# A residual block on one core: 36 scalings go from VectorE to ScalarE, with a new order of operations

## The chip, the core and the metric

The kernel runs on one core of a Trainium2 chip. The core has a matrix engine (TensorE, in the profile PE, with its weight loads as PEld), VectorE (DVE), ScalarE (ACT), GpSimd (POOL) and SyncE (SP), which issues most DMAs here. Each engine works through its own instructions in the order in which they were written, and waits on semaphores for the others. The metric is the device time of one execution in microseconds (us), the median of several runs. The profile is of one execution.

## What is computed

A residual block of a diffusion model, on x of shape (2, 512, 64, 64) in bfloat16:

```
def conv3(z, w):                     # 3x3, padded by 1, 512 -> 512 channels
    zp = jnp.pad(z, ((0, 0), (0, 0), (1, 1), (1, 1)))
    taps = [jnp.einsum("bchw,oc->bohw", zp[:, :, i:i+H, j:j+W], w[:, :, i, j])
            for i in range(3) for j in range(3)]
    ...
h = conv3(_silu(gn(x, g1, be1)), w1)
emb = _silu(t_emb) @ w_emb
h = h + emb.reshape(B, C, 1, 1)
h = conv3(_silu(gn(h, g2, be2)), w2)
return x + h
```

gn is a group normalization with 4 groups of 128 channels.

## The kernel before

**Stages.** A convolution ("layer") is done in chunks: layer, image and half of the rows. So there are eight, chunks 0 to 3 for the first convolution (two images, two halves) and 4 to 7 for the second. Each chunk has four units, one for each 128 output channels; `unit(c, k)` (line 818) writes unit k of chunk c, called u00 to u73 below, 32 in all.

**Input side.** For each chunk and each of the four input channel tiles, `load_a` (645) brings the half image (name a), `silu` (669) applies normalization and SiLU on ACT, and `rows_a` (680) and `rows_b` (694) form "row planes", sums and differences of every fourth row, mostly on DVE (names k, row and rob, with chunk and tile: rob23 is tile 3 of chunk 2). This saves multiplications: a convolution over rows is computed from six products, s = 0 to 5, in place of twelve. From chunk 1 on columns are treated likewise ("nested" products, A and B matmuls over 256 columns, beside plain ones over 512). Products of the following chunk's planes are formed while the units of this chunk run. The planes lie in two sets of buffers, one for each of two chunks.

**Output side.** PE sums the products of a unit in PSUM banks. ACT moves them to SBUF (`evac_o`, `evac_m`, `evac_pair`, `evac_b`, lines 842 to 858; names o4, o5, m0 to m3, b). DVE then adds the halves (names S and A), and the end of `unit` (1002 to 1015) turns four products into four rows:

```
tt(tw(SD, 1024), M(0, 2), M(2, 2), AD, nm + "s")
tt(M(0, 2), M(2, 2), M(0, 2), SB_, nm + "d")
se = CFG["s"][c]
scal(se[0], M(2), M(1), 8.0, nm + "8")
scal(se[1], M(3), M(1), 2.0, nm + "2")
scal(se[2], A(SD + 512, [[1, 512]]), A(SD + 1024, [[1, 512]]), 4.0, nm + "4")
```

The sums s and d, then three scalings by 8, 2 and 4 (128x512 elements each), then the additions y, on DVE. `scal` (373) takes ScalarE (`act`, line 371 in the profile) or VectorE (`ts`, line 352), as `CFG["s"]` says for each chunk. An accumulating DMA on POOL adds the outer rows (name oa). In the first layer the unit goes to a scratch tensor in DRAM (st), is squared and summed on ACT (sq), and `gn2` makes the second normalization's scale; in the second layer it is added by DMA to a copy of x in the output (names out and pre).

**Other work.** `prep_w1` and `prep_w2` make the transformed weights with scalings on ACT and sums on DVE, `fetch_w2` and `stream_w2` bring them; `emb` is the small matmul of the embedding; `stats1` sums and squares the second image on ACT (st10 to st13, in chunk 0). At the start `warm` and `fill` are matmuls whose results are not used, and st00 to st03 are the statistics of the first image.

**The order.** Nothing is emitted directly. Each helper records an operation in a `Plan` with its engine, the regions it reads and writes and so the operations before it. `ORDER` (168) is a string of 2753 two-character numbers, one for each operation, and `emit` (97) writes the operations in that order. The DMAs on SP and the work on POOL stand in it too, and each engine takes its operations in the sequence that results. So all instructions of the helpers have one line each in the profile: L348 is a DVE sum or difference, L352 a DVE scaling, L371 an operation of ACT, L386 a DMA, L390 a memset, L401 a matmul.

Of the kernel before, what the change touches and what calls it, by code (L numbers as in the profile page):

```python
# [165 lines left out]


ORDER = (
    "0D0E0F0G0H0I0R0S0T0U0W2T1u0v0y1Q2J1N2c3F1r2M0c0X0a0Z0Y0d0e0f00010b020g13030h14150i0j0k0l0L0m170n0N16180405061907"
    "081X1Y1Z1A1_0o1a1c0K1B0M1C1D0p0O1E1b1F1d0q0r1e0s1f0_1g1G1H2021231I1h090A0B0V0C3K1i0J22240t0u0w250x0z1j1J2610271k"  # L170
    "2e12281K292U1l2A1T2B1m1n112C1o2D1x2E2F1U2G1y2P1z1-1W0-1L1M1O1P1R1S1p1q1s1t1v1w2H2I2K2L2N2O3C3D3E3L0Q2Q1V2R2S0P3M"
    "4g2W2l2X2m2Y2n3G2Z4T3g4L2f3O2i3P3N3Q2h3S3R2g3V2a3H3a3W3U2o2p3h3i2q2r2s2t2u2v2w2x2y2z3j2-3u4M2d2j4N2k2_304U2b3Z32"
    "314O5P3X3k3c3d3b5H3Y3T4h4P5I4Q5J4k4V334X4W4Y344Z35364b374a3e4S4R3f384d4m4e4n4f6Y4j3v3w3x3y3z3-3_4243443l45464748"
    "494q4r4s4t3m41404B5Q4A6L4i4c5K6D5L5M6F6M6E4u4v3n3o4w4x4-4_50515253543p555c5d5e5f5h2V4l6Z5R3r6a5T7u5U5S5V3q5W5X7v"
    "5Z5a4p3s5N4C3t3I4D4G4F4E7w4H5b8y4o3J56395Y6GB7B84I3A4z574y3B6IB96H5g586N596P5B5C6O5A6Q5D6RBB6T6SBABD6U6K6W6J6X8z"
    "5O6V5i5j5k5l5m5n5o5r5s5t5u5w5x5y5z5-5_60616b6c6d6e6g5v5q5p6h6i6j6k6l6m6n6s6t6u6v6x6y6z6-6_70717262767763BC4JBN7h"
    "BF6fBP4KBH648-65A0686766BJA169A2BR5E8lBOBGBED56A5F6w7P78797A6o7B7C7D7x7y7z7-5G6p8081BQ828384858687BI74737EDDB47Q"
    "6q7RB57S6r7T7UB67V757W7XBL7FD7DF7YBK7ZBS7aBT7b7G7c7d7H7e7K7f7J7g7i8988D66BDEBM7ID97LDH7j7l8A7m7k7n8B7o7pD27tDL7M"
    "BUEeDN8C8D8EDG7_8F8H8I8J8K8L8M8N8O8S8T8U8V8W8X8Y8Z8_908GD88Q8P91929495969798999A9B9G9H9I9J9L9M9N9O9P9Q9R9S8a9W9X"
    "8m8b7O9p9q6CD37r8RD4DIDB7sDA8cDJ7N7q8d8n8f8p8o8q8g8r8e9C9D8t8s8hDP8v9KEgDKDMDC93DOEfEh9UAt9FEi9EDRDQ9T8x8w9V9Y9Z"  # L180
    "9a9b9c9d9f9eA3A4A5A6A8A9AAABACADAEAFAKALAMANAPAQARASATAUAVAWAaAbAcAdAeAfAgAhEm8u9r9t9s9u9v9w9x8iEuEo9gEjAG9hEqEn"
    "GB9yCrEwA7EpAHAuAO8kEk9k9j9-9i9_9l9zAXCsAYAiAjAvAIAxAwAyAJAzA-A_AZB0B2B3AkCQAlAoAnAmCRCtEvDSEl8jApEO9m9nAqCvB1Cw"
    "CuCxCTCyCzBVBWBXBYBaBbBcBdBZBiGDBjBeBfBgBhBlBmBnBoBtBuBvBwByBzB-B_C0C1C2C3C6C7C8C9CCCDCECFDTDUDVDW9oBkDYDZDaDbBp"
    "BqExBsEbEyEcCUBrEdE-EsErBxEPC5C4AsCAGJCGD0CVCSEzCWCBD1CHC_CIDcDdDeDfDjDkDlCXCYDmDrDsDtDuDwDXDhGLDgDxDyDzD-D_E0E1"
    "E4E5E6E7EAEBECEDF0F1F2F3FxEtE_GCGKDiCKCLG8CJC-G9GFGNCMCZGAArGRCaEQGEESERETGHEUGGEWEVDnDoDvGTGMFyE8E2E3EEGPDpDqCb"
    "EYE9GVHhHUHVGSHjGIEFEJEaCcEGEZEHGOCNCOEXHpHiGQGUF5F6F7F8F9FAFBFCFGFHFIFJFOFPFQFRFTFUFVFWFXFYFDEIGXHlCdGWEKCeFzFE"
    "FKFLF4HrFFHkHxHzFbFZFaFdFcFeFfFgFhFjFkFlFmGZGaGbGcGeGfGgGhGiGjGkGlFSGpGqGrGsGxGyGzG-H0H1H2H3FnH4H5H6H7HqGYHsCPF_"
    "CfG0F-G1CgG3G2ChFMFNCiHtCjFiCkG5FoHvClFpCmG7HmFqFsGmI3FrGuGoGtGnI5J6ELJ7G4HuHnFtG6HyHoI7GvHWKNGdHAHBHCHDHGHHHIHJ"
    "IBICH8ENH9FuI4EMHYHXHZH_HaCnCpHbCoHcGwCqHdHgHfHEG_HFHeHKI6KPJ8J9HwH-KONMNLFvHLIDIEIGIHIIIJIKILIMINIRISITIUIZIaIb"
    "IPIOIFIcIeIfIgIhIiIjIkIlIoIpIqIrIuIvIwIxIQJSJTJUJVJXJYJZJaI8HMIWHPHOIVI0HNI1I9JAHQIXIYImInIsJCJBJDJEItJFJGJJKQIy"  # L190
    "IdIzJHKRI-JKJIJ1IALeLfI2HRJLLgFwMvJ0KTI_KUKSJ2KVKWKXJMNJMwMxHSJWJgJfJbJcJdJeJiJjJkJlJqJrJsJtJmJhO-OzJvJwJxJyJzJ-"
    "J_K0K3JnNKK1K4K5K6K9KAKBKCKjKkKlKmKoKpKqKrKsKtKuKvKzK-K_L0JuK2KbKYLhLiJpJ3KaKZJNJoK7HTKDJ4QBQAOkJOLjLkJPLlLmK8Lo"
    "KELnKnKFKIKGKHLqLpKJKxL1KyKwMyL2MzLsL4L3JQM_KKN0OiOjL5L6L7L8LALBLCLDOxL9LELFLGLHLKLLLMLNLQLRLSLTLOLILJL-L_M0M1M3"
    "M4M5M6M7M8M9MAMEMFMGMHMMMNMOMPMRLUMSMTMUMVMWMXMYMbMcMdMeLPLrLVM-JRLWKcJ5N1M2MDMIMCMBN2LXLYLZN3LaKdKMMJMLMZMaMfN4"
    "N6MKN7MgLbPvRMKLPxRNPwLtOyMQOlMhMiMjMkNNNONPNQNSNTNUMlNVNWNXNYNZNbOHMmOmNRLdKeMnMqOIMoMpKfMrKgMsN5OKOoOLKhOpNaMu"
    "NcNdNeNgNhNiNjNkNlNmNnNrNsNtNuNvNwNxNyN-N_O0O1O2O3O4O5O_P0OqOMKiOnOJLuNoNpOrONP1P2P4NzP5P6P7NfOOOsLvOuNqLwOtPyP3"
    "O6LcSYQ8R7NFR5OPOwO7LxPzSZMtQ9TkR6N8P8P9PAPBPDPEPFPGTlP_R8O8OCPCNHQ0LyO9P-SHNGOBQ1LzRLRKOAPIPJPKPLPMPNPOPPPTPUPV"
    "PWPXPYPZPaPcPdPePfPgPhPiPHPQPjQCQDQEQFQHQIQJQKOvODQ2Q3PSPRPbPkQ4PlN9PmNAPnQLQMQNQOQQQRQSQTQVQWQXQYQZQaQbQcQgQhQP"
    "QiQjQkQlQmQnQpQqQrQsQtR9NBQ7RBRANCOFOEOGSJSIUwUxPpQGPoQUSKSWTTRCTVTUSXNINDRDPqQdQuQvQwRORPRQRRRTRUQ5NEQ6PrPtQoQx"
    "RVRWRXRYRZRaRcRdReRfRhRiRjRkRlRmRnRoPsREQfRFQeRGRHRbSLRJRITiW7SNSMSOSPRgRSQySQQzSRQ-SSSVUfTjUgUhPuRpR1Q_R0SUR2Rs"  # L200
    "RtRuRvRwRxRyRzR_S0S1S2S3S4S5S6SaXJSbS7R-ScSdSfSgShSiSjSkSlSmSoSpSqSrStSuSvSwSxSySzS-OQSTT2T3T4T5T6T7T8R3R4ORRqRr"
    "OSSnS8OTS9OUSAOVOWOXOYOZOaObSDSCSBSEOcOdOeOgS_OfT1OhSeT9TBTCTDTETFTGTHTITmTnToTpTrTsTtTATJTWSsT0TKTLTXTZTMTaTOTb"
    "TNUiTuTvTwTxTyT-T_U0U1U3U4U5U6U7U8U9UAUEUFUGTzUHUIUJUKULUNUOUPUQUBSFTqU2XIUvUuURUSUTUUUyUzU-U_V1V2V3V4V5V6V7V8VA"
    "VBVCVDTYYXSGW6YYVtTPTcTdTQUMVFVGVHVIUVVJVKVLVMVQVRVSVTTeTgUjUDTfUlUCUkUmUnUWThUXUoUpUbUqUYUsVrVsVuV9X1W5TRW4XGX3"
    "X2UaUZVNVvUrVxVwUtUcVyVPYFZnXHZmV0YDVEVUVVVWVXVZVaVbVcVdVeVfVgW8W9WAWBWDWEWFWGWHWIWJWKWMWNWOVYVzVhX4UdTSYEb0a_Ue"
    "YGWPWRWSWTWUWVWWWXWYWcWdWCYWWQVOWLWeWfWgWhWiWjWlWmWnWoWpWqWrWsXKXLWZV_V-ViW0W3X5VjX7W2X6X8W1VkZSZUX9VlVmXBXAVnXC"
    "YHXFXEVoYJWkWtWaWbYKYIYLXDWuYMWvYNWwWzVpYVZTajcKcLXMXNXPXQXRXSXTXUXVXWXYXZXaXbXdXeXfXgXhXiXjXkXoXpXqXXXrXsXtXuXv"
    "XxXyXzX-X_Y0Y1Y2ZVXcXOWxWyXlYQW-YOXmXnY3XwYUY4YRZWY5ZYY6YTYPZZZXahZlVqZkaiakY7Y9Y8ZaYZYaYbYcdcW_YeYfYgYhYiYjYkYl"
    "YnYoYpYqYsYtYuYvYwYxYyYzZ1Z2Z3Z4YmZ5Z6Z7Z8ZAZBZCZDZEZFY-YdZGZHZoZpZqZrZtbwdba-byX0bxazYAYBZ9YrZuZvZwZxZyZzZ-a0a1"
    "a2a3a5a6a7a8a9etesZIaAaBaCaGaHYCZbZcY_Z0ZdZgZJZiZKalanZLZeaobzaIaJaKaLaMaNZ_aPaQaRZMaSaTaUaVaWZNZOaDZsa4ZjapZfam"  # L210
    "ZPaXaOarZhaqaEaFasauaYavb-aZc0aab_atc1acabadaeZQb1b2b3b4b6b7b8b9bAbBbCbDbFbGbHbIbKbLbMbNbObPbQbRbVbWbXbYbEc2ayaf"
    "cDc4c3YSc7c8cCc6bZbabbbSbJcHbcbdbebfbgbhbibjbkblcMcNbmcOcPcQcRcScTcVcWcXcYcZcacbcccgchcicjckclbTbUcUcEbncGcIbocF"
    "c5cJbpdTgvdUZRaxcBcAc9awb5cdbrbscmcncpcqcrcsctcucvcwczc-c_d0bqbtcod1d2d3d4d9dAdBdCdDdEdFdGdddedfdgcxdhdidjdkdmdn"
    "dodpdqdrdHdsdtdxdydzd-d5dId_e0e1e2dVcfcedWdYdldXdae4e5e6e7e8e9eAdZeBeEeFeGeHd6agekcydKd8d7dLdNdJdMdOemdPeobuelep"
    "erendRdQeqbvdueIeJeKeLeQeReSeTeUeVeWe3eXeuevewexeyeze-e_eCf1f2f3f4eMeYeNdvdweZf0ePdSeDebeOeaecedeeefegehf5f6f7f8"
    "fCfDfEfFfGfHfIfJfLfMfNfOfPfQfRfSf9fKfTeifBfAfUfsfwftfVfWfXfYfZfafbfcfhfifjfkflfmfnfog1g2g3g4g5g6g7g8gAgBgCgDfdfe"
    "fpfqfvg9gEgFgGgHgLgMejf_g0gNgOgPgQgRgSgUgVgWgXgYgZgagbgegfggghgjgkglgmfgfffrgIfufxfzfygJgTgcgKgdgogpgsgqgrf-gign"
    "gugtgwgygxg_h0gzg-"
# [1172 lines left out]
```

## Time and profile before

| | |
|---|---|
| median of 3 runs | 461.7 us (460.53 to 462.13) |
| profiled execution: time, span | 461.67 us, 459.9 us |
| PE matmuls, busy | 445.3 us, 97% |
| DVE busy | 440.9 us, 96% |
| ACT busy | 377.3 us, 82% |
| POOL busy | 65.8 us, 14% |
| DMA | 94.89 MB, mean 206 GB/s |
| last matmul ends, DVE ends | 454.6 us, 456.6 us |

The span goes from the first to the last instruction. Matmul ends are modelled by the profiler, so PE's busy time is no measure of how well it is used; the starts of its matmuls are. Waits are put down to the operation that came last. An instruction's duration includes a part in which the following one may already run, so the distance between two starts can be shorter than a duration.

### The profile page before, as it was taken

The page shows a single profiled execution, that of the slowest core. Times are in us where ns is not written, and L with a number is a line of the kernel's source. Part 1 is how long each engine was busy: PE and PEld are TensorE (multiplying, and loading weights), DVE is VectorE, ACT ScalarE, POOL GpSimd, SP SyncE. Part 2 cuts the span into 40 slices and gives each one's busy share as a digit, 9 for nine tenths or more (in the row PEclk, how much of TensorE's full clock was granted, in tenths as well). Part 3 has the DMA queues.
Part 4 walks back from the last instruction along what each step waited for, and adds up shares of the span by engine and source line. Part 5 has one row for each costly group of instructions (what it writes and reads, how often), then busy time and mean ns, then how long its engine had stood idle before and what let it go on. Part 6 is the DMA issues. An engine that isn't in the chain of part 4 may idle for free. (4 is left out here: it accounts for less than half of the span.)

```text
span 459.9 us, 8113 instructions
## 1 busy us (share of the span) xinstructions
PE 445.3 (97%) x2891; PEld 280.4 (61%) x2891; DVE 440.9 (96%) x842; ACT 377.3 (82%) x571; POOL 65.8 (14%) x91
## 2 busy tenths in 40 slices
...
PEclk9999999999999999999999999999999999999999
...
GB/s 319 383 218 152 191 227 72 167 249 213 214 149 232 124 255 205 212 197 193 351 264 261 251 324 198 165 213 204 152 191 254 242 219 209 156 194 115 154 73 93
DMA packets 44472, 94.89 MB, mean 206 GB/s; under 512 B 6544, under 2 KB 18192, under 8 KB 44432
## 3 DMA queue, kind: packets, MB, share of 16 engines
...
q8 instruction: 22, 0.36, 0.3%
q14 instruction: 18, 0.15, 0.1%
...
HBM read 62.25 MB, written 31.32 MB: 203 GB/s over the span
## 5 line engine op out<-in xcount | busy, mean ns | idle before, releaser
L401 PE MATMUL psum<-ar 128*128 128x256 f16 (+2 forms) x2771 | 427.7, 316 | 6.8 <-DVE ar L348 4.4
L348 DVE TENSOR_TENSOR ar<-ar 128x1040 f16<-128x1040 f16 (+8 forms) x621 | 409.0, 717 | 7.6 <-ACT ar L371 4.2
L401 PEld LDWEIGHTS <-ar 128*128 128x128 f16 (+1 forms) x2763 | 268.1, 98 | 163.0 <-issue 11.7
L371 ACT ACTIVATE ar<-psum 128x512 f16<-128x512 f32 (+4 forms) x250 | 158.7, 679 | 34.8 <-DVE ar L348 16.4
L371 ACT ACTIVATE ar<-ar 128x512 f16<-128x512 f16 (+6 forms) x146 | 158.9, 1116 | 32.3 <-DVE ar L348 26.0
L371 ACT ACTIVATE ar<-ar,fs 128x2112 f16<-128x2112 bf16 (+1 forms) x32 | 68.8, 2151 | 6.1 <-DVE fs L498 3.0
L386 POOL DMA_DIRECT2D ar<-ar x35 | 38.2, 1111 | 193.0 <-DVE ar L348 78.1
L352 DVE TENSOR_SCALAR ar<-ar 128x512 f16<-128x512 f16 (+3 forms) x90 | 31.5, 370 | 0.4 <-issue 0.2
L386 POOL DMA_DIRECT2D out_dram<-ar x15 | 19.0, 1265 | 52.6 <-DMA ar<-ar 27.2
L371 ACT ACTIVATION_READ_ACCUMULATOR ar<-psum 128x1 f32 x104 | 22.2, 213 | 0.0
L390 POOL MEMSET ar<- 128x65 f16 (+4 forms) x29 | 5.3, 216 | 117.4 <-DVE ar L348 76.8
L401 PEld LDWEIGHTS <-ones_bf 128*128 128x128 bf16 x75 | 7.3, 103 | 6.2 <-issue 3.5
L401 PE MATMUL psum<-ar,ones_bf 128*128 128x260 bf16 x56 | 7.3, 275 | 1.1 <-DMA ar<-in_x_dram 0.9
L401 PE MATMUL psum<-ones_bf 128*128 128x512 bf16 x19 | 6.3, 466 | 1.1 <-DVE ones_bf L405 1.1
L371 ACT ACTIVATION_READ_ACCUMULATOR ar<-ar 128x1 f32 x36 | 7.3, 201 | 0.0
L479 POOL TENSOR_TENSOR fs<-fs 128x1 f32<-128x1 f32 x4 | 3.7, 917 | 18.0 <-DVE fs L477 18.0
L401 PEld LDWEIGHTS psum<-fs,ones_neg 128*128 128x128 f32 x36 | 4.7, 191 | 1.8 <-ACT ar L371 0.9
L401 PE MATMUL psum<-fs,ones_neg 128*128 128x1 f32 (+3 forms) x36 | 4.7, 244 | 0.3 <-ACT ar L371 0.3
L439 ACT ACTIVATE s_sb<-tparm 128x18 bf16<-128x18 bf16 x1 | 0.2, 218 | 3.2 <-DMA tparm<-in_t_emb_dram 3.2
L438 DVE CAST fs<-gparm 128x16 f32<-128x16 bf16 x1 | 0.2, 175 | 2.7 <-DMA gparm<-in_params_dram 2.7
L401 PE MATMUL psum<-ar,s_sb 128*2 128x512 bf16 x9 | 2.7, 377 | 0.0
L433 ACT ACT_TABLE_LOAD x1 | 1.3, 1283 | 1.7 <-PEq L1375 1.7
...
## 6 DMA issues: line engine op xcount, KB each, us to landing
...
```

The source lines that it names most:

```text
L348: pl.op("DVE", 0.075 + 0.000521 * out.n, lambda: nc.vector.tensor_tensor(out=out.ap, in0=a.ap, in1=b.ap, op=op), regs(a, b), regs(out), name)
L352: pl.op("DVE", cost or 0.075 + 0.00026 * out.n, lambda: nc.vector.tensor_scalar(out=out.ap, in0=a.ap, scalar1=s, scalar2=None, op0=ALU.mul ...
L371: lambda: nc.scalar.activation(out=out.ap, in_=a.ap, func=func, scale=sc, **kw), regs(*rr), regs(*ww), name)
L386: lambda: eng.dma_start(out=out, in_=in_, **kw), regs(*r), regs(*w), name, lat=3.2 if sw else None, after=after, sw=sw, seq=seq)
L390: pl.op("POOL" if eng == "gpsimd" else "DVE", 0.08 + 0.0005 * out.n, lambda: e.memset(out.ap, v), (), regs(out), name)
L401: nc.tensor.matmul(out.ap, lhsT=lhsT.ap, rhs=rhs.ap, start=st, stop=sp, skip_group_check=True)
L433: nc.scalar.activation(out=fs[:, WARM:WARM + 1], in_=fs[:, WARM + 1:WARM + 2], func=ACT.Silu)
L438: nc.vector.tensor_copy(out=fs[:, GB:GB + 4 * CT], in_=gparm[:])
L439: nc.scalar.activation(out=s_sb[:], in_=tparm[:], func=ACT.Silu)
L479: pl.op("POOL", 0.85, lambda: nc.gpsimd.tensor_tensor(out=F(rs, n).ap, in0=N.ap, in1=F(NEGH, n).ap, op=ALU.pow), regs(N), regs(F(rs, n)), ...
```

## The change

It changes two constants. In `CFG["s"]` the entries of chunks 0, 1 and 3 go from DVE to ACT, three scalings in each of 12 units, 36 operations:

```
-    's': (('DVE', 'DVE', 'DVE'), ('DVE', 'DVE', 'DVE'), ('DVE', 'ACT', 'ACT'), ('DVE', 'DVE', 'DVE'), ('ACT', 'ACT', 'ACT'), ('ACT', 'ACT', 'DVE'), ('ACT', 'ACT', 'ACT'), ('DVE', 'ACT', 'DVE')),
+    's': (('ACT', 'ACT', 'ACT'), ('ACT', 'ACT', 'ACT'), ('DVE', 'ACT', 'ACT'), ('ACT', 'ACT', 'ACT'), ('ACT', 'ACT', 'ACT'), ('ACT', 'ACT', 'DVE'), ('ACT', 'ACT', 'ACT'), ('DVE', 'ACT', 'DVE')),
```

And `ORDER` is another sequence of the same 2753 operations, found by a search in which each kind of transfer had a measured lateness. The operations, what each of them reads and writes, and what must precede it are the same. Its first line shows how it reads:

```
-    "0D0E0F0G0H0I0R0S0T0U0W2T1u0v0y1Q2J1N2c3F1r2M0c0X0a0Z0Y0d0e0f00010b020g13030h14150i0j0k0l0L0m170n0N16180405061907"
+    "0D0E0F0G0H0I0R0S0T0U0y2M0v0W1u2J1Q1N0A0C090B2c3F3C1r3K0c0001020304050607080X0Y0a0Z0b0g0d0e0f0h0i0j0k0l0m0n0V2T13"
...
```

By engine, among the operations that stay on it, 53 of PE's 1208 stand at another place, 671 of DVE's, 330 of ACT's, 175 of SP's 213 DMAs and 42 of POOL's 83.

More of the change, by code (lines that the diff above doesn't have):

```diff
@@ L168 @@
 ORDER = (
-    "0D0E0F0G0H0I0R0S0T0U0W2T1u0v0y1Q2J1N2c3F1r2M0c0X0a0Z0Y0d0e0f00010b020g13030h14150i0j0k0l0L0m170n0N16180405061907"
[L170 to L218, printed above, removed]
+    "0D0E0F0G0H0I0R0S0T0U0y2M0v0W1u2J1Q1N0A0C090B2c3F3C1r3K0c0001020304050607080X0Y0a0Z0b0g0d0e0f0h0i0j0k0l0m0n0V2T13"
@@ new lines @@
+    "161415180L0K17190M1A0o1B0p1C0r1D0q1E0s1X1Y1Z1F0N1b1a1c0t1_1d200u210w0x1G22240J0_101e0O1f1g1H1J1h1i231j1k3H251I1K"
+    "26271128292U1l122A2B2C1n1m1o1T2D1x2F2E1y2G0P1-1z1U2P1V1W3G3D3E0z0-1L1M1O1P1R1S1p1q1s1t1v1w2H2I2K2L2N2O2X2W2l2m2Y"
+    "0Q2n2Q3J3I3L2Z4g4O4T2V2R2S2o3M3N3O3P3Q3S2f3R2h2i3a3W3V2e2g3U4P2d4Q4U2a3g3h3i2p2q2r2s2t2u2v2w2x2y2z3j2-2_2b4L2k2j"
+    "3u3v3w3x3y3z3-5K3k3X3T3230314V334X344Y4W4M4Z4b4R4a4d4f4e3d3c5L4N4S3Z3b4k5P3l3_42434445464748493m3n4q4r4s4t4u4v4w"
+    "4x6L5H3o3Y373536383f5Q40415I4h4c5R3r3e5T5S4-3p3q4_505152533s54555U5V5X4m5W4B5J4j4A5M4l3t4n4C4D6Y5N5a6Z5Z4i4G4F4E"
@@ new lines @@
+    "5c5d5e5f5h5i5j5k396D6G3A5Y4p4H6M6E6F4z4y3B56577hB7B85O6N5b6H6a4I4J5g6P6O6Q8l6R4o7u7v7w6T6S586X6W598y6V6U8zB9BB5l"
+    "5m5n5o5r5s5t5u5w5x5y5z5v5C5A5B5D6JBA6I8-5q5pA0BDBCBNBPA1BR6K625-5_60616b6c6d6e6g6364656h6i6j6k6l6m6n6s6t6u6v6x6y"
+    "6z6-6_7071727677786w6f687P797A7B7C7DBF66BH674KBOBGDD5EBI7E6o6pBEBQA2B4B57Q7R7S7TBJB6697U7VBK7W6q7XBL7F7473D57YBS"
+    "7Z6rBT7aDFD7757b7G7c7HDH7d7e7f7gD95G7K7I7J5FBM7LD2D37iD6DEBU6A6B7x7y7z7-80818283848586878C8D8E8F8H8I8J8K898G887_"
+    "D88L8M8N8O8S8T8U8V8W8X8Y8Z8_90919294959697DG8Q8P8aEe7M8m8b7j7l7k7m8B7n7o7p8A7t7rD48RDBDADI7qDL9p7NDC8c7s8d8nDJEf"
@@ new lines @@
+    "DM8p8o8q8rEgDN6C8g8e8f7O9CAt8t8s8h8v8u8wEiDP8x9qDO98999A9B9G9H9I9J9D9L939E9KEh9M9N9O9T9P9Q9R9S9W9X9Y9Z9a9b9c9dA3"
+    "A4A5A69U9eA8A9AAABACADAEAFAKAL9fAMANAPAQARASATAUAVAWAaAbAcAdAeAfAgAhAu9FDQDR8iDKEuDS8k9r9t9s9u9v9V9w9x9g9z9hEj9-"
+    "9k9i9jEnEmAGA7AHEoEp9y8jCr9l9_AvAJAxAwAYAOAXAyAIAzAZA_A-B0B3B2CsAjEwAiCtAkAlAoAmAnCvCuCQApEO9mBVBWBX9oCwCRB1CTCx"
+    "EkEqEbEyCzCyBYBZBaBbBcBdBeBfBgBhBjBiBlBmBkBnBoBtBuBvBwByBzB-B_C0C1C2C3C6C7C8C9CCCDCECFDTBqBpBrBxDUDVDWElEvCUEcD1"
+    "EdBsCVErEPEsAqGJGB9nEtAsExCSC_CWCAGLC5C4DYDZDaDbDcDdDeDfDjDkCXE-EzD0GCCGGDGNCBCYCHG8CZCIGFG9CJCaGACbDgGKC-EQESER"
@@ new lines @@
+    "CLDXGEGMDiDhCKGGCcETCMFxGRE_HhCNArEUGHGPGOFyEVCdDlDmDrDsDtDuDwDxDyDzD-D_E0E1E4E5E6E7EAEBECEDF0F1F2F3DoDnF5F6F7F8"
+    "DvE2E3E8F9FAFBFCFGFHFIFJFOFPHjEEGTEWDpDqHlCeE9CfEFGSHiGIF4FDCgGVEGChEZCiEXGQHUHpFFFEHkGUGXFLEIFKEJEaEHFzCjGWEKHq"
+    "HxCkEYF_ClF-G0FQFRFTFUFVFWFXFYFZFaFdFeFfFgFjFkFlFmGZGaGbGcGeGfGgGhGiGjGkFbGlGpFSFcGqGrFhCPHrHsFnCOELGYJ8FMG1FNG2"
+    "HnG3HtCmFiG7FoHmHVHzEMHyHoG4FpH_HuGsGxGyGzG-H0H1H2H3H4H5H6H7HAHBHCGmGnGdHDHGHHHIHJIBICGoFsFrHWG_FqHvG5G6FtGtH8Gu"
+    "KNJ6J7HYCnHZHXCoHaGwHbCpHcI4I3HwCqHdHfHEH-ENHKH9FuKOJ9FvNLKPI5GvHgIDIEIGIHIIIJNMIKILIMINIRISITIUIZIaHFI1HLI6I7IF"
@@ new lines @@
+    "HMIPIOIWIQIVHPHOI8I0HNI9HeHQIXIYJAJCJDIbIcIeIfIgIhIdIiIjIkIlIoIpIqIrIuIvIwIxJSJTJUJVJXJYJZJaImIsInJbJcJdJeJiJjJk"
+    "JlJqJrJsJtJvJwJxJyJzJ-J_JEKQIyJBItJGJFJHJJJIKRFwHRIzI-KTJ0J1I_KSJKKUJ2LgJgK0K3K4K5K6JfK9KAKBKCKVJWJmJnJhK1K2JuK7"
+    "LeI2JLLfIAKXKWJ3KaJpJMJNJoKYLhKjKkKlKmKoKpKqKrKsKtKuKvKzK-K_L0L5L6L7L8LALBLCLDLELFLGLHKDLKLLLMLNLiHTK8KbKEJOLkKZ"
+    "LjLlKFL2KIKwLmMvMxMwHSNKQBQAKcNHOiL1MyKxKGKnKHKyJPLnJQLoJRLrLpKJKdKKL9MzLILQLRLSLTL-L_M0M1M3M4M5M6M7M8M9MALJMEMF"
+    "MGMHMMMNMOMPMRMSMTMULOMVMWLUL3KeL4M2MCJ4NJMBMXMYMbMcMdMeMhMiMjMkNNNONPLsM-M_LqJ5N0LPKfOxOjOkRMPvLtPwOyRNKLPxN1KM"
@@ new lines @@
+    "N8LVKgLWLZLXLYN3N2KhN4LaMIMJMQMfMDMaMZN6MKMLN7MgLbOlMlMmOHMnOIN5OmOoOpMqMpNQNSNTNUNVNWNXNYNZNbNcNdNeNgNhNiMoLdNR"
+    "OqOKMrOnMsNaMuKiNfNjNkNlNmNnNrNsNtNuNvNwNxNyN-N_O0O1O2O3O4O5O_P0P1NoO6NzOsOrLuOLLvOMOJLwONOtNpNqLxNINFNGR5O7P2P4"
+    "P5P6P7OOOPP8P9PAPBPDPEPFPGPIPJPKPLOwO8LyO9LzOvQ9LcTkTlR6PyPzOCOBP_OQOuP3Q0MtQ8PCOAODPHPMPNPOPPPTPUPVPQPWPXPYPZPa"
+    "PcPdPePfPgPhPiPjQCQDQEQFQHQIQJQKQLQMQNQOQ1PbQQQRQSQTQVQWQXQYQZPkQaQbQcQgQhQiQjQkO-R7OEOFOzP-SHSIOGSJR8N9PRPSNAPl"
+    "Q2Q3ORPmQ4NBPnQ5NCR9RBQ7QPPpQUPoPqQGQ6NDRCRAQdPrRDRFNEREQfQeSKRKRLQlQmQnQpQqQrQsQtQuQvQwRORPRQRRRTRURVRWRXRYRZRa"
```

19 lines of the change are left out of this document (added).

## The prediction

> **What bounds the kernel now.** First the page: the engines' shares, and the granted clock over the 40 slices.
>
> ```profile
> span 459.9 us, 8113 instructions
> ...
> PE 445.3 (97%) x2891; PEld 280.4 (61%) x2891; DVE 440.9 (96%) x842; ACT 377.3 (82%) x571; POOL 65.8 (14%) x91
> ...
> PEclk9999999999999999999999999999999999999999
> ```
>
> Two engines are almost always at work, and the clock is full. Work, not one chain, sets the end; so I ask of each stage which engine has idle time. Stages are cut at the ends of chunks: chunk 0 is 34.5 to 90 us, chunk 1 to 148, 2 to 203, 3 to 256, 4 to 308, 5 to 360, 6 to 408. Columns of the windows view: stretch, length, then the busy time of PE, PEld, DVE, ACT and POOL.
>
> ```profile
> 34.50:90.00 55.50, 55.50 (x250) 23.50 (x248) 54.45 (x100) 54.30 (x74) 5.75 (x7) 1.00 0.57 162
> 90.00:148.00 58.00, 57.60 (x327) 31.96 (x326) 56.19 (x127) 47.01 (x94) 8.33 (x8) 1.00 0.74 208
> 148.00:203.00 55.00, 53.31 (x339) 33.07 (x338) 54.76 (x124) 51.16 (x107) 7.82 (x9) 1.00 0.71 198
> 203.00:256.00 53.00, 53.00 (x337) 32.88 (x336) 52.72 (x87) 49.67 (x101) 1.91 (x6) 1.00 0.81 272
> 256.00:308.00 52.00, 51.02 (x362) 35.29 (x361) 51.76 (x86) 42.86 (x47) 6.80 (x13) 1.00 0.76 216
> 308.00:360.00 52.00, 50.81 (x358) 34.74 (x357) 51.13 (x89) 38.43 (x46) 10.23 (x12) 1.00 0.83 212
> 360.00:408.00 48.00, 47.83 (x346) 33.73 (x345) 47.79 (x73) 39.35 (x42) 10.67 (x11) 1.00 0.82 204
> 408.00:455.00 47.00, 44.54 (x376) 36.43 (x374) 43.95 (x82) 28.18 (x39) 7.83 (x7) 1.00 0.65 114
> ```
>
> DVE has no reserve from 148 us on (0.2 to 0.9 us of 48 to 55 idle). ACT's idle time is small in chunks 0 to 3, 1.2 + 11.0 + 3.8 + 3.3 = 19.4 us, and 9 to 14 us in each later chunk. Who makes PE wait, between 34.5 and 455 us:
>
> ```profile
> PE psum L401 <- DVE ar L348: 4.1, 6, 1.6
> PE psum L401 <- ACT ar L371: 1.3, 3, 0.7
> PE psum L401 <- DVE fs L469: 0.8, 1, 0.8
> ```
>
> Matmul ends are modelled, so I also took PE's starts: a 512-column matmul follows the next at 213 ns, a 256-column one at 107 ns, and every distance more than 0.15 us over that is a wait. Up to 34.5 us two waits on row planes (25.7 and 29.9 us) make 0.65. Through chunk 3 there are four: 0.15, 0.57 (90.5, an evacuation by ACT), 1.79 (151.4, the row plane rob23 by DVE) and 0.24, together 2.75 us. After that twelve make 6.42 us: mostly row planes of DVE at the start of a chunk, and three evacuations that ACT could not start while DVE still read their buffers. The largest, at the start of chunk 7:
>
> ```profile
> 409.85 7.04 PE L401 MATMUL psum<-ar 128*128 128x256 f16 x63 [1.22 <-DVE ar L348]
> 417.27 0.61 PE L401 MATMUL psum<-ar 128*128 128x256 f16 x2 [0.38 <-DVE ar L348]
> 418.24 3.97 PE L401 MATMUL psum<-ar 128*128 128x256 f16 x33 [0.36 <-DVE ar L348]
> ```
>
> So 9.8 us of waits can be won at most, nearly all owed by DVE. The rest (matmuls, 5.3 us after the last one, the loads at the start) the change does not touch.
>
> **The change, part by part.** It moves 36 scalings of 128x512, and puts much of the order anew.
>
> ```profile
> L371 ACT ACTIVATE ar<-ar 128x512 f16<-128x512 f16 x44 | 26.1, 626 | 19.0 <-DVE ar L348 18.2 <-DVE fs L469 0.5 <-DVE fs L489 0.2
> L352 DVE TENSOR_SCALAR ar<-ar 128x512 f16<-128x512 f16 x52 | 13.3, 283 | 0.1
> ```
>
> *Removed from DVE.* An instruction takes 283 ns, but the next starts 0.20 us after it in the timeline: 36 x 0.203 = 7.3 us, 2.4 in each of chunks 0, 1 and 3. DVE is full, so this counts.
>
> *Added to ACT.* The same operation takes 626 ns there, and 0.53 us from start to start: 36 x 0.53 = 19.1 us; at the full 626 ns it is 22.5. I take 19.1, since ACT will be packed. Chunk 0 gets 6.4 us where 1.2 are idle, chunk 1 6.4 for 11.0, chunk 3 6.4 for 3.3: together 19.1 for 19.4. ACT becomes the fullest engine up to 256 us.
>
> *Does the order move other ACT work out of the way?* I read both orders and summed, for chosen results, the start-to-start times of all that stands ahead on the engine. Ahead of the u02 and u03 evacuations that free PE's next banks (u02m2, u03o4) six scalings were put in, but two other evacuations or a square and a weight scaling out: +2.1 and +0.8 us. With ACT idle for 10.1 us in the first 34.5 as now (by the loop's own operations), and never after, they come 0.25 and 0.46 us before PE needs them at its present times. But ahead of u40b, the first paired evacuation of chunk 4, stand all 36 scalings and nothing has gone: +19.6 us. It begins at 264.5 now, after 21.2 us of idle time since 34.5. Thus ACT may idle only 1.6 us in those 230 and still be there; PE needs its bank 1.1 us later. ACT's waits now are 4.2 us on DVE's planes, 4.1 on issue, 3.9 on PE, 3.5 on the mean and variance chain, 2.2 on loads and 0.8 on a scaling. A later ACT finds most of these ready; I keep 3 of the 19, in place of bounds of 0 and 19. It is then 3.0 - 2.7 = 0.3 us late for PE at u40. I therefore count nothing won through chunk 3: the 2.75 us of waits come back as waits on ACT, and 0.3 more.
>
> *What DVE keeps.* Its scalings' results now come from ACT, and it waits in order behind them: the sums put u02s 2.7 us, u03s 0.8, the u10 sums 1.8 and k20 (after silu20) 1.1 us after DVE is ready, 6.4 in all; DVE idles 1.05 + 1.81 = 2.9 us in chunks 0 and 1 now. So 3.5 of its 7.3 us go, and it enters chunk 4 ahead by 3.8. Of the later waits of PE, 6.42 us, that many go. Ahead of the planes PE waits for, DVE's list is shorter by 5.2 (rob23), 7.2 (rob53), 6 to 7 (rob63), 9 to 11 (rob73) and 7 to 12 us (ok2, ok3), so the head start reaches them.
>
> *The order.* PE changes 53 of 1208 places (by at most 7), DVE 671, ACT 330, SP 175 of 213 DMAs, POOL 42 of 83. Start: the first ten loads keep their order. The eight filling matmuls, spread over 4.8 to 13.7 us, now stand ahead of the statistics: 8 x 0.21 = 1.7 us from 4.85, until 6.55, where the first statistics ran at 6.17; the loads to 17.0 hide that. st01's last matmul is some 0.7 us later, row00 some 2 us earlier since two weight preparations went behind it, one square (1.95 + 0.2) goes into ACT's gap of 2.0 us before silu03. Between -0.65 (both early waits go) and +0.7: I take 0. POOL: a60's border memset, at 289.6 now, stands behind u41's accumulating output, thus after 302.0; its load, at 293.5, behind it on SP, and behind that pre50, pre53, a61 and a weight stream at 300.3. silu60 runs at 321.6, the weights' first use near 320.7: covered by over 10 us. a40's memset goes from 184.5 behind a41's at 199.2, its load lands near 204 for silu40 at 205.1, and u40 is 50 us off. The copies of x to the output go back by up to 24 places, all landing well before the accumulating store. None costs while these covers last; a load later by 1 us than its cover costs as much. In chunk 0, at the two margins of 0.25 and 0.46, I add 0.5.
>
> **The sum:** 0 + 0.3 + 0.5 - 3.8 = -3.0 us. The profiled execution took 461.67 (span 459.9 and 1.8 around it), the median of the runs is 461.7: **458.7 us**.
>
> **Rivals.**
>
> *ACT is the new bound (slower).* Place: chunks 0 to 3; price: each us that ACT idles there over 2.7 is PE's; it decides from 6.0 us (6.0 - 2.7 + 0.5 - 3.8 = 0). For it: 19.1 us for 19.4 idle; no stage of the trace has ACT above 98% (54.30 of 55.50). Against: DVE keeps 99% from 148 to 256. If half of the 19.4 stays idle, 9.7 - 2.7 = 7.0 us late at u40, plus the 0.5, and of PE's later waits only the 3.0 us go that DVE causes after 360: +4.5, **466.2**; at 626 ns each 3.4 more. [...]
>
> *All of DVE's time is won.* ACT's waits vanish as it comes later: 7.3 us and 0.65 at the start, **453.7**. For it: ACT's waits each are at most 3.0 us. Against: the sums for u02s to k20.
>
> *It comes to nothing.* ACT idles 5 to 7 us, or loads and stores eat the gain: **461.7**.
>
> *The clock falls at the start.* The fills no longer stand between the statistics. By the sums PE's longest gap there is 1.4 us (7.4 to 8.8). After its last matmul (454.6) the clock record goes to half 3.3 us later. A gap that long would run what follows at half speed, as the first matmuls do (0.43 us against 0.21, for some 3 us): +1.7, 460.4 from the forecast. [...]
>
> **Chances.** A measurement here tells about 0.3% (1.4 us) from no change. Forecast (456 to 460.3) 0.42; all won 0.11; nothing 0.14; ACT's bound 0.30; clock, on top of small losses, 0.03. Faster 0.53, same 0.14, slower 0.33. Range 453.5 to 466.5: 0.04 below, 0.10 above, where ACT keeps over half its idle time.
>
> **What would show it.** Right: ACT busy over 98% in chunks 0 to 3 with its idle time falling from 19.4 to about 3 us; DVE's busy time 433 to 434; u40 at its present time within 1 us; the waits at 307 to 418 us cut by half or more. Wrong: PE waits on ACT of over 3 us before 270 (ACT's bound); waits on DVE unchanged after 300 (DVE has lost all its head start); a clock row below 9 in the first slices; ACT's scalings far from 0.53 us apart.

## The result and the profile after

The changed kernel takes 465.53 us (median of 5, 463.97 to 466.57), the kernel before 461.07 beside it. The ratio is 1.0092, with a 95% interval of 1.0066 to 1.0119: slower by 4.5 us, where 3.0 us faster were forecast. The page of the changed kernel, profiled in the slowest of these executions (466.57 us):

```profile
span 464.8 us, 8111 instructions
...
PE 446.0 (96%) x2891; PEld 280.7 (60%) x2891; DVE 438.9 (94%) x806; ACT 393.7 (85%) x607; POOL 66.0 (14%) x91
...
PEclk9999999999999999999999999999999999999999
```

VectorE has 36 instructions fewer and is busy only 2.0 us less; ScalarE has them, and is busy 16.4 us more. The clock is full. The windows view, with the columns that the prediction names:

```profile
34.50:90.00 55.50, 55.18 (x248) 23.33 (x247) 54.22 (x94) 55.37 (x76) 5.71 (x6) 1.00 0.67 188
90.00:148.00 58.00, 58.00 (x330) 32.18 (x329) 55.33 (x113) 54.60 (x110) 8.85 (x8) 1.00 0.68 184
148.00:203.00 55.00, 53.73 (x343) 33.29 (x341) 51.38 (x114) 50.14 (x104) 6.29 (x6) 1.00 0.69 189
203.00:256.00 53.00, 49.81 (x312) 30.31 (x311) 52.55 (x85) 52.86 (x104) 3.43 (x9) 1.00 0.81 263
256.00:308.00 52.00, 50.45 (x352) 34.15 (x350) 51.19 (x83) 47.49 (x62) 5.99 (x11) 1.00 0.66 202
```

The third row is the odd one: between 148 and 203 us ScalarE, which should have no time left, idles 4.9 us (55.00 less 50.14), and VectorE, full before (54.76), idles 3.6. In the fourth TensorE loses 3.2. Who makes TensorE wait between 34.5 and 455 us (total, times, longest):

```profile
PE psum L401 <- DVE ar L348: 5.2, 5, 2.8
PE psum L401 <- ACT ar L371: 4.6, 5, 1.5
```

Before these were 4.1 and 1.3 (and 0.8 for L469). By the starts of the units, against the kernel before, TensorE is 1.6 us late at u10 and u20, 1.0 at u30, 4.5 at u31, 4.7 at u40, and 4.5 at the end. Two steps, at the very start and in chunk 3, make the whole loss.

**The start.** TensorE's timeline from 4 us on in the changed kernel (start, time, engine, line, operation, how many), and the first statistics of the kernel before:

```profile
3.60 4.56 PE L401 MATMUL psum<-ones_bf 128*128 128x512 bf16 x13
8.00 1.06 PE L401 MATMUL psum<-ar,ones_bf 128*128 128x260 bf16 x8
```

```profile
6.17 1.06 PE L401 MATMUL psum<-ar,ones_bf 128*128 128x260 bf16 x8 [0.94 <-DMA ar<-in_x_dram]
```

The eight fills now run in one piece with the last five matmuls of warm. Every profiled execution begins at half clock. Up to the turn of the clock (to full at 6.81 us in this execution, at 3.92 in the one of before) a fill takes 0.43 us from start to start and then 0.21, so the fills run from 5.73 and the first statistics start at 8.00 where they started at 6.17. st01's last sums come at 14.38 (12.74), silu01 at 20.6 (18.0).

**Chunk 3.** ScalarE's and VectorE's timelines; the bracket is the idle time ahead, and what ended it:

```profile
189.36 2.00 ACT L371 ACTIVATE ar<-ar 128x2145 f16<-128x2145 f16 x1 [3.81 <-DMA ar<-ar]
```

```profile
191.38 0.70 DVE L348 TENSOR_TENSOR ar<-ar 128x1040 f16<-128x1040 f16 x1 [3.32 <-ACT ar L371]
```

The first is k32, the scaling for tile 2 of chunk 3's planes. It writes the buffer that va31, an accumulating transfer issued by GpSimd, still reads. va31 goes out at 179.96 and lands at 189.33: 9.4 us, 4.2 before. The view of transfers (how many, size, time to landing) has a33, the load of tile 3, and va31 in after, then va31 in before:

```profile
ar<-in_x_dram SPq DMA_DIRECT2D x1, 552.5 KB, 7.9
ar<-ar POOLq DMA_DIRECT2D x1, 260.0 KB, 9.4
```

```profile
ar<-ar POOLq DMA_DIRECT2D x1, 260.0 KB, 4.2
```

VectorE's row32 needs k32, rob33 ends at 208.98 (204.71), and TensorE waits:

```profile
209.03 1.48 PE L401 MATMUL psum<-ar 128*128 128x512 f16 x9 [2.80 <-DVE ar L348]
```

What stands beside va31 is on SP: a33, issued 0.16 us ahead of it, and a store of w2_22 0.54 us ahead of that. The issues in after, then in before:

```profile
179.80 0.87 SPq L386 DMA_DIRECT2D ar<-in_x_dram  x1
179.96 0.91 POOL L386 DMA_DIRECT2D ar<-ar  x1 [2.05 <-ACT ar L371]
```

```profile
174.13 0.33 SPq L386 DMA_DIRECT2D ar<-in_x_dram  x1
177.41 0.91 POOL L386 DMA_DIRECT2D ar<-ar  x1 [4.43 <-DMA ar<-in_x_dram]
```

### The profile page after: what moved, and what is told of

It is laid out like the page before. It is cut to its first block, busy times and chain, and to the rows that moved or that the text cites. A ratio compares the mean times of both kernels' runs of the same rounds, so it can differ in the third digit from the quotient of the medians.

```text
span 464.8 us, 8111 instructions
## 1 busy us (share of the span) xinstructions
PE 446.0 (96%) x2891; PEld 280.7 (60%) x2891; DVE 438.9 (94%) x806; ACT 393.7 (85%) x607; POOL 66.0 (14%) x91
## 5 line engine op out<-in xcount | busy, mean ns | idle before, releaser
L401 PE MATMUL psum<-ar 128*128 128x256 f16 (+3 forms) x2771 | 427.4, 316 | 10.6 <-DVE ar L348 5.2
L348 DVE TENSOR_TENSOR ar<-ar 128x1024 f16<-128x1024 f16 (+9 forms) x621 | 410.4, 719 | 10.3 <-ACT ar L371 6.1
L371 ACT ACTIVATE ar<-ar 128x512 f16<-128x512 f16 (+6 forms) x182 | 179.6, 1031 | 35.6 <-DVE ar L348 30.7
L352 DVE TENSOR_SCALAR ar<-ar 128x520 f16<-128x520 f16 (+3 forms) x54 | 23.2, 440 | 0.9 <-ACT ar L371 0.4
L371 ACT ACTIVATION_READ_ACCUMULATOR ar<-psum 128x1 f32 x104 | 24.1, 232 | 0.0
L390 POOL MEMSET ar<- 128x65 f16 (+4 forms) x29 | 6.4, 264 | 90.4 <-DVE ar L348 44.4
```

The lines of the kernel that those rows point to most:

```text
L348: pl.op("DVE", 0.075 + 0.000521 * out.n, lambda: nc.vector.tensor_tensor(out=out.ap, in0=a.ap, in1=b.ap, op=op), regs(a, b), regs(out), name)
L352: pl.op("DVE", cost or 0.075 + 0.00026 * out.n, lambda: nc.vector.tensor_scalar(out=out.ap, in0=a.ap, scalar1=s, scalar2=None, op0=ALU.mul ...
L371: lambda: nc.scalar.activation(out=out.ap, in_=a.ap, func=func, scale=sc, **kw), regs(*rr), regs(*ww), name)
L390: pl.op("POOL" if eng == "gpsimd" else "DVE", 0.08 + 0.0005 * out.n, lambda: e.memset(out.ap, v), (), regs(out), name)
L401: nc.tensor.matmul(out.ap, lhsT=lhsT.ap, rhs=rhs.ap, start=st, stop=sp, skip_group_check=True)
```

## The experiments

Beside each group of runs the kernel before ran too (medians 460.6 to 461.0); ratios are to that. Operations have the names of the prediction's text, and the letters of the theories are those of the recorded expectations.

**The two parts of the change, alone.** x1 is the new order with the old table; x2 the old order with the new one.

```
x1:  ORDER of after; 's' of before
x2:  ORDER of before; 's' of after
```

> The new order, with all 36 scalings back on VectorE. Theory A (ScalarE has too much to do in chunks 0 to 3): ScalarE has 19 us less there and is no longer late, VectorE has 7.3 us more; PE starts u40 within 1 us of the kernel before and the time is 460 to 462.5. Theory B (the places in the new order do it: the fills ahead of the statistics, and k33 behind the accumulating transfer va32): the lateness at the start (1.6 us) and at u30 (3.5 us) stays, and VectorE's 7.3 us come on top: 466 to 471.

> The old order, with the 36 scalings on ScalarE. Theory A: ScalarE gets 19 us into chunks 0 to 3 without anything moved out of the way, and PE waits for it already in chunk 0; 467 to 478, worse than the change as a whole. Theory B: the old places keep the start and u30 on time, and VectorE has 7.3 us less: 458 to 461.5.

x1: 470.69, 1.0210 [1.0195, 1.0226]. x2: 483.32, 1.0486 [1.0469, 1.0503]. Neither part does anything good by itself: x1 came out in theory B's range, x2 above even theory A's. In one and the same order the scalings are worth 470.7 - 465.5 = 5.2 us; without an order that makes room they cost 22. The new order alone costs 9.7. Falls of the clock are part of these sums: x2's execution stands at half clock for five stretches of 3.41 us, up to 8.5 of its 22 us, and x1's for one, from 10.63 us, ahead of the first scaling. So some 1.7 of the 5.2 need not belong to the scalings.

**The two places.** x3 puts TensorE's first operations back in their old sequence; x5 moves one load on SP.

```
x3, TensorE:  -warm fill*8 st00 st00 st01 ...
              +warm fill st00 fill st01 fill st00 st01 st01 fill*3 st01 fill*2 ...
x5, SP:       -w2_22 a33 w2_31 w2_31 w2_32
              +w2_22 w2_31 w2_31 a33 w2_32
x7:           both
```

> The changed kernel, but with TensorE's first operations (fills and statistics, up to the third tile's) in the sequence of the kernel before; all else as changed. Theory B: the 1.6 us that u10 starts late go, 463.5 to 464.5, and no wait of 0.7 us or more is left on TensorE between 9 and 15 us. Theory A: ScalarE, full in chunk 0, uses up what is won by chunk 2, and the time stays at 465 to 466.

> The changed kernel, with one load moved: a33 (x for tile 3 of chunk 3) is issued on SP after w2_31's second load, some 7 us later, so that it no longer runs beside the accumulating transfer va31. Theory C (va31, 9.4 us against 4.2 before because it shares the queues with a33, holds k32 on ScalarE for 3.8 us, and VectorE and then TensorE behind it): va31 takes 4 to 6 us, ScalarE's wait at 189 us goes, TensorE's wait at u30 falls from 3.5 to under 1.5, u40b comes 2 to 4 us earlier, and the time is 461.5 to 463.5. Theory A (ScalarE simply has too much to do): TensorE is as late at u40 as in the changed kernel (4.7 us, within 1), and the time stays at 465 to 466.

> The changed kernel with both places put right: TensorE's first operations in the sequence of the kernel before, and a33 issued later. If the two places are what the change lost by, the gains add up: 1.9 and 2 to 4 us off 465.5, 459.5 to 461.5, no slower than the kernel before. If ScalarE's load is the cause, TensorE is late at u40 again by 2 us and more, and it stays at 463 to 464.

x3: 463.64, 1.0055 [1.0041, 1.0068], so 1.9 us. x5: 462.26, 1.0033 [1.0020, 1.0045], so 3.3. x7: 460.97, 1.0005 [0.9996, 1.0014]: no difference from before that can be measured. With a33 behind (x5) va31 takes 6.1 us, k32 starts at 185.21 in place of 189.36 and rob33 ends at 204.82; 0.8 of these 4.2 us is a shorter loss at the start of that execution. In x5 ScalarE's wait ahead of k32 is

```profile
185.21 2.00 ACT L371 ACTIVATE ar<-ar 128x2145 f16<-128x2145 f16 x1 [0.48 <-DMA ar<-ar]
```

and in x3 the statistics start at 6.21 between the fills:

```profile
6.21 1.05 PE L401 MATMUL psum<-ar,ones_bf 128*128 128x260 bf16 x8 [0.98 <-DMA ar<-in_x_dram]
7.10 0.38 PE L401 MATMUL psum<-ones_bf 128*128 128x512 bf16 x1
```

In x7 the clock turned at 7.08, later than in after, and u10 was on time all the same. So the loss against the kernel before belongs to two places of the order; the 36 scalings are still on ScalarE in x7. The gain that was forecast is missing there too.

**Around the transfer, without the load.** x4 and x6 take operations of chunk 3's planes from GpSimd's DMA to VectorE.

```
-    'vacc': (0, 3, 3, 3, 0, 0, 0, 0),
+    'vacc': (0, 3, 3, 2, 0, 0, 0, 0),      # x4: va32 on VectorE
+    'vacc': (0, 3, 3, 1, 0, 0, 0, 0),      # x6: va31 and va32
```

> The changed kernel, but the sum va32 (row planes of tile 2 of chunk 3) is done by VectorE and not by an accumulating transfer, so that k33 on ScalarE has no transfer to wait for. Theory B: the 3.8 us wait of ScalarE at 189 us goes, TensorE's wait at u30 falls from 3.5 to under 1 us, and the time falls by 2.5 to 3.5, to 462 to 463. Theory A: ScalarE is as late at u40 as before, since it has to do as much as before, and what is won at u30 is lost there: 465 to 466.5.

> The changed kernel, with the sums va31 and va32 on VectorE in place of the accumulating transfers (1.3 us more on VectorE). Theory C: k32 waits for nothing, and the time is 462.5 to 464.5, TensorE's wait at u30 under 2 us. Theory A: VectorE's 1.3 us come on top: 466 to 467.5.

x4: 464.81, 1.0087 [1.0068, 1.0106]. That was the wrong transfer: k32 waits for va31, and it still did (va31 took 9.5 us), and TensorE waited 3.7 us for rob33. x6: 463.39, 1.0061 [1.0048, 1.0074], 2.1 us under after, with VectorE doing the sum itself.

**Less for ScalarE.** x8 puts chunk 0's 12 scalings back on VectorE.

```
-    's': (('ACT', 'ACT', 'ACT'), ...
+    's': (('DVE', 'DVE', 'DVE'), ...
```

> The changed kernel, with the 12 scalings of chunk 0 back on VectorE. Theory A: ScalarE is full in chunk 0 (0.1 us idle of 55.5), so 6.4 us less there let it catch up: PE up to 1 us earlier at u10, 463 to 465. Theory C: ScalarE's load in chunk 0 costs nothing, since evacuations come ahead of the scalings; VectorE gets 2.4 us more, which it has no room for, and the time rises to 466.5 to 468.5.

x8: 464.82, 1.0087 [1.0074, 1.0101], within the interval of the changed kernel, in theory A's range and out of theory C's. A third of the load gone changes nothing that can be measured: no support for ScalarE as the bound, and no proof against it. u10 is only 0.6 us late in its execution, but the clock turned early there (at 4.76), which accounts for that (see "The start failed" below).

**The load beside the transfer, in the kernel before.**

```
SP:  -a33 w2_23 w2_21 u20st w2_31
     +w2_23 w2_21 u20st a33 w2_31
```

> The kernel before with one load moved: a33 (128x2210, 0.57 MB), on SP two stores and one write of u20 later, so that it is issued about 176.6 instead of 174.1, just ahead of the accumulating transfer va31 (issued 177.4). Theory C (a large load issued just ahead of va31 slows it, and the scaling k32 behind it holds ScalarE, VectorE and TensorE): va31 takes 7 to 9 us for 4.2, k32 ends 2 to 4 us later, and TensorE loses 1.5 to 3.5 us by u31: 462.3 to 464.3. Rival (va31 is slow in the changed kernel for what else moves there, its stores above all): va31 within 1 us of 4.2 and the time within 0.5 of before.

x12: 464.40, 1.0080 [1.0067, 1.0092], just above theory C's range, yet not by its way. va31 took 6.7 us (4.2 before), less than expected, and ScalarE was held by the load itself, which silu33 reads at this place of the old row:

```profile
181.61 2.15 ACT L371 ACTIVATE ar<-ar,fs 128x2112 f16<-128x2112 bf16 x1 [4.56 <-DMA ar<-in_x_dram]
```

It shows that a33's place is worth 3.6 us there as well, not that the two transfers are to blame.

**Where the gain went, first try.** x7's waits of TensorE from 260 us on:

```profile
PE psum L401 <- ACT ar L371: 4.1, 4, 1.5
PE psum L401 <- DVE ar L348: 0.7, 2, 0.4
```

Counted by starts, those of 0.4 us and more after 264 us are 4.7 us before, 6.0 in after and 5.8 in x7. What the forecast sold as less waiting had turned into waits for evacuations. x9 puts five of them earlier in ScalarE's row, x10 adds u40b, x11 is x10 with the scalings on VectorE.

```
x9, ScalarE:  u53b ahead of u528 u522 silu70;  u63b u63b ahead of u628 u622;  u70b u70b ahead of u634
x10:          also u32sq u33sq behind u40b u40b; VectorE: row50 behind u33O
x11:          x10 with 's' of before
```

> The kernel with both places mended (x7), with five evacuations put earlier in ScalarE's row alone: u53b ahead of the weight scalings u528 and u522 and of silu70, both u63b ahead of u628, both u70b ahead of u634. In x7 their operands were ready 7.0, 5.5 and 3.2 us before they ran, while ScalarE idled 1.9, 1.25 and 2.8 us just ahead, and TensorE waited 1.50, 0.69 and 0.90 us for them. Theory P (VectorE's time is won, and lost again on places of evacuations in ScalarE's row): those 3.1 us go, 457.5 to 458.5, and VectorE's waits at rob63 and ow0 stay within 1 us. Theory Q (VectorE's supply sets the late stages, as the prediction's working had it without the head start): the waits come back as waits for rob63, ow0 or rob73, 460.5 to 461.3.

> x9, and at u40: the squares u32sq and u33sq behind both evacuations u40b on ScalarE, and row50's second operation behind u33O on VectorE. In x7 TensorE waited 1.71 us for u40b, which ran at 267.13 behind u32sq (1.97 us) and behind u33O, done 266.87. Theory P: u40b by 0.7 to 1.0 us earlier and as much off the time, 456.7 to 457.7. Theory Q: within 0.4 of x9, for the wait moves to u41 or rob50.

> x10 with the 36 scalings of the change back on VectorE, in the same places of the order. Theory P (the scalings on ScalarE are worth time where the order fits them): VectorE has 1.4 us more in each chunk 0, 1 and 3 and again its late supply, and the time is 4 to 6 us over x10 (the same edit on the changed kernel gave 470.7 for 465.5): 461 to 464. If ScalarE's load in chunks 0, 1 and 3 costs what VectorE saves, as the prediction's rival had it, the two are within 1 us.

x9: 463.07, 1.0052 [1.0039, 1.0066]. x10: 467.07, 1.0127 [1.0109, 1.0144]. x11: 471.92, 1.0241 [1.0221, 1.0261]. Theory P fell, and theory Q named the waits of x9 but not its time. In x9 the evacuations come in time, and TensorE waits as long for VectorE, from 260 us on:

```profile
PE psum L401 <- DVE ar L348: 4.0, 3, 2.2
PE psum L401 <- ACT ar L371: 1.6, 1, 1.6
```

Its profiled execution took 461.42 us, like x7's 461.29; the other four took 463.0 to 463.3 at a mean granted clock of 0.993 to 0.994, against 0.998: by that, an estimated 4 us at half clock each. x10 undid itself: the squares that I moved feed gn2's statistics, and TensorE waits at u41, after which the clock is at half from 277.67 to 281.08:

```profile
273.98 1.03 PE L401 MATMUL psum<-ar 128*128 128x256 f16 x8
277.14 7.08 PE L401 MATMUL psum<-ar 128*128 128x512 f16 x36 [2.13 <-DVE fs L469]
```

**Second try: VectorE's own row.** By operations, its instructions in x7 occupy 7.2 us less for the 36 scalings, and 4.9 us more for the rest: planes (rob) 1.4, statistics 1.0, sums d 0.7, and so on. (An operation is counted from its start, or from the end of the one ahead if that is later, to its end.) The sum of their durations grew by 0.6 us only. In all traces an operation starts some 0.08 us before the end of the one ahead, but 0.035 us after it where it needs that one's result. Two timelines of VectorE show it, first x7, then x13:

```profile
40.39 0.72 DVE L352 TENSOR_SCALAR ar<-ar 128x2145 f16<-128x2145 f16 x1
41.15 2.18 DVE L348 TENSOR_TENSOR ar<-ar 128x1040 f16<-128x1040 f16 x3
```

```profile
39.85 0.72 DVE L352 TENSOR_SCALAR ar<-ar 128x2145 f16<-128x2145 f16 x1
40.49 3.65 DVE L348 TENSOR_TENSOR ar<-ar 128x1040 f16<-128x1040 f16 x5
```

The scaling is k10 in both. In x7 row10, which reads it, comes next: 40.39 + 0.72 = 41.11, and it starts at 41.15. In x13 a sum of another tile stands between, and starts at 40.49, 0.08 before k10's end. The old row has 40 such pairs, the new one 81 (x1, with the scalings on VectorE, 84); 25 of the 41 more lie between 34.5 and 148 us in x7. From start to start that is 41 x 0.115 = 4.7 us. The 4.9 us above leave the 0.035 us out: of them the pairs make 41 x 0.08 = 3.3, two thirds. A wait on an older result shows no such cost in x7: 277 operations wait there for VectorE's own semaphore, but not for the operation directly ahead, and they start 0.08 us before its end like those that wait for none. A wait on the operation directly ahead costs the 0.115 us (0.08 + 0.035).

```
x13, VectorE:  x7 with 33 pairs parted, such as
               -rob03 rob03 k10 row10
               +rob03 rob03 st10 k10 rob01 row10
x14:           x13 with 's' of before
x15, VectorE:  before with 40 neighbours exchanged, 38 more pairs
```

> The kernel with both places mended (x7), with 33 pairs of neighbours in VectorE's row parted: where an operation stands right behind the one whose result it reads, another operation is put between the two; all other engines keep their rows. In the traces such an operation starts 0.04 us after the end of the one ahead, any other 0.075 before it, so a pair costs 0.115 us. The row before has 40 such pairs, the new one 81: 41 x 0.115 = 4.7 us, two thirds of the 7.2 us that the 36 scalings leave free. Theory R (these pairs are where VectorE's gain went): the row gets 33 x 0.115 = 3.8 us shorter, 2.4 of it before 148 us, and of TensorE's 5.8 us of waits after 264 some 2 go: 458 to 459.5. Theory S (VectorE's supply is not what sets the late waits): the row gets shorter all the same, and the time stays 460.5 to 461.5. Where waits join into one over 2 us the clock may fall, for 1.7 us.

> x13 with the 36 scalings of the change back on VectorE, in the same order. What the scalings are worth once the order fits them: theory R 36 x 0.203 = 7.3 us more on VectorE, less what it idles there, 3 to 7 us over x13, so 461.5 to 466. If the order alone made the loss and the scalings nothing, within 1 us of x13.

> The kernel before, with 40 neighbours exchanged in VectorE's row between 34.5 and 203 us, so that 38 more operations stand right behind the one whose result they read (78 pairs for 40), each exchange within the margin that other engines leave; all other rows are as before. Theory R: 38 x 0.115 = 4.4 us more on VectorE, which idles 2.9 us in chunks 0 and 1 and 0.5 in 2 and 3: 462.5 to 465.5. Theory S: 460.3 to 461.3, the row longer and no more.

x15: 464.70, 1.0082 [1.0068, 1.0096]; VectorE is busy 2.6 us longer and TensorE waits 2.78 us for rob23 at 150.3, where it waited 1.79, and 0.6 longer at u10; the clock is at half from 153.20 to 156.61. So pairs cost time where VectorE is full, though the 40 exchanges moved operations too. x13: 460.72, 1.0000 [0.9991, 1.0008]. Theory R's range is missed, theory S's holds. VectorE did get its time back:

```profile
PE 445.1 (97%) x2891; PEld 280.6 (61%) x2891; DVE 436.4 (95%) x806; ACT 394.1 (86%) x607; POOL 65.8 (14%) x91
```

It is 2.2 us less busy than in x7 (438.6), and idles 1.7 us more; the time is the same within the intervals. Its windows from 360 us on leave VectorE 3.9 us idle, where x7 leaves 3.1, and TensorE waits for evacuations again. x14: 466.09, 1.0115 [1.0100, 1.0130]: in this order, too, the scalings are worth 5.4 us (x10 and x11: 4.9). Again a fall of the clock is part of it: x14's execution has one, x13's none, and x11's one more than x10's.

**Both rows at once.** x16 and x17 fit the rows of VectorE and ScalarE (x16: TensorE's too) to the durations of x13's trace; the rows of the queues stay.

```
x17:  x13 with other places for VectorE's and ScalarE's operations after 36 us
x16:  x17's fit carried on, with TensorE's operations too
```

> x13 with the rows of VectorE, ScalarE and TensorE fitted anew against its own trace: the durations of x13's profile, 0.115 us for an operation right behind the one it reads, transfers as long as measured and also a quarter longer. The rows of SP and GpSimd stay. x13 had TensorE wait 5.7 us after 264 us (u40b 1.48, rob63 0.57, u53b 1.50, u63b 0.78, u70b 0.90, ow0 0.44), on evacuations and on planes by turns. Theory T (these waits belong to the places in two rows at once: ScalarE's alone, in x9, and VectorE's alone, in x13, left them): the sum goes to some 4 us, and the time is 1.0 to 1.8 us under x13, 459.0 to 459.8. Theory S (what is left is the work itself or transfers): within 0.4 of 460.7. A wait over 2 us may cost the clock's fall, 1.7 us.

> The same with TensorE's row left as in x13: VectorE's and ScalarE's rows alone fitted anew. Theory T: 0.6 to 1.2 us under x13, 459.5 to 460.1. Theory S: within 0.4 of 460.7.

x16: 466.21, 1.0132 [1.0113, 1.0152]. x17: 466.98, 1.0140 [1.0117, 1.0163]. Both theories missed. In x17 another accumulating transfer, va21, took 8.3 us where it took 4.8 in x7; VectorE waited 3.3 us for it, and TensorE for rob23:

```profile
154.36 7.99 PE L401 MATMUL psum<-ar 128*128 128x512 f16 x35 [4.10 <-DVE ar L348]
```

So an order that leans on the durations of one trace can change those durations (va21: 4.8 to 8.3 us); what lengthened va21 was not shown. In x16 va21 took 4.6 us, and TensorE still waited 3.6 us for rob23, after VectorE had waited 2.6 us for ScalarE at 106.5; the cause was not followed up. Three of its five executions had no fall of the clock (0.999 to 1.000) and took 465.9 to 466.2 us.

## Why the prediction was wrong

*The price of the scalings was right.* 36 of them take 7.2 us from VectorE (7.3 forecast), and on ScalarE they take 19.3 us from start to start (19.1 forecast). Three pairs of kernels in three orders put their worth at 4.9 to 5.4 us, falls of the clock included.

*The start failed.* "8 x 0.21 = 1.7 us from 4.85, until 6.55" and "the loads to 17.0 hide that" took the fills at full clock. With the clock turning at 6.81, warm and the first three fills ran at half, and the fills ended at 8.00; the loads did not hide it, since st01's sums and silu01 wait for TensorE: 1.6 us at u10, and x3 gives 1.9 back. How much it is, the turn of the clock decides. With this start u10 is late by 0.8 us where the clock turned at 5.15 and 5.20 (x5, x4), 1.3 at 6.24 (x6) and 1.6 at 6.81, about half a microsecond for each that the turn comes later; x8's 0.6 at 4.76 lies on that line. With the old start it is within 0.2 of before for turns from 3.94 to 7.08 (x3, x7, x9, x13). So the +0.7 that the prediction gave as its worst case holds for an early turn only.

*"I keep 3 of the 19" failed.* ScalarE keeps 8.5 us idle in chunks 0 to 3 (0.13 + 3.40 + 4.86 + 0.14), 3.8 of them in one wait. I priced ScalarE's waits on transfers at 2.2 us from the old trace, and of the new order's transfers looked at loads that come late by themselves (a60, a40), not at one load that lengthens another transfer. With the start and a33 put right (x7) the sum is 6.1 us and u40 starts on time, though TensorE still waits 1.7 us for u40b (0.3 forecast).

*"It enters chunk 4 ahead by 3.8" failed.* The sum took VectorE's other work as unchanged in 671 new places. It grew by 4.9 us, two thirds of it the pairs, which the old trace could have told: the operations behind scalings and sums there start 0.035 us after their end or 0.08 before it. In after, VectorE also idles 8.0 us between 34.5 and 256 (3.4 before), 3.3 of it for k32. (The prediction's readings of idle time, 9 to 14 us for ScalarE in each later chunk and 0.2 to 0.9 for VectorE from chunk 2 on, leave out the last row, with 18.8 and 3.1; nothing in the sum hangs on that.)

*"Of the later waits of PE, 6.42 us, that many go" failed, and not for that reason alone.* With VectorE's time given back (x13) the waits stay, for evacuations; with the evacuations moved (x9) they are for planes. What can be said is that these 5.8 us hang on both rows; that they can be won together was not shown: x17 ran into a longer transfer, and x16 waited longer at several places, rob23 above all, for causes not found. This stays open.

*The rival "ACT is the new bound" named the size, 466.2, and the place, but the size by luck.* Its terms were 7.5 us late at u40 and 3.0 won behind it; measured are 4.7 and 0.1. Its rule is near in after: 8.5 - 2.7 = 5.8 us at u40 by it; 4.7 measured at u40 (1.6 of them from the start), 6.4 at u41. In x7 it fails: 6.1 - 2.7 = 3.4 by it, nothing measured at u40, 1.6 at u41. And its cause, the load on ScalarE, does not explain the loss: x7 has the same load and loses nothing, and x8 with a third less gains nothing. Which engine is better for the scalings depends on the order: VectorE costs some 5 us more in the new one (x1 against after, x14 against x13), ScalarE 22 more in the old one (x2).

*The rival "The clock falls at the start"* did not happen in the changed kernel, but in x1's execution, at half from 10.63 to 14.04, with 1.5 us of gaps. The 1.4 us that the prediction computed are close to that. The price of 1.7 us fits a fall of 3.41 us at half clock, as the runs have it; the "some 3 us" of the prediction make 1.5.
